# Windowed attention and a GEGLU feed-forward block on one core: residue-class attention with short key blocks, on-chip reciprocals, 512-token FFN chunks, engines ordered by hand

## The chip, the core and the metric

The kernel runs on one core of a Trainium2 chip. The core has a matrix engine (TensorE, PE in the profile, with PEld for its weight loads), three engines for elementwise work (VectorE = DVE, ScalarE = ACT, GpSimd = POOL), a queue engine (SyncE = SP) and 16 DMA engines. Each engine works its own instruction list in order and waits for others by semaphores. TensorE writes only into PSUM, eight banks of 512 float32 per partition; VectorE and ScalarE read it from there. The metric is the device time of one execution in microseconds, lower is better.

## The reference

Attention over 8 batches, 8 heads, 576 positions and 64 channels, then a gated feed-forward block over the 4608 tokens:

```python
window = 32; dilation = 4; scale = 1.0 / np.sqrt(D)
scores = scale * np.matmul(q, k.transpose(0, 1, 3, 2))
rel = pos[:, None] - pos[None, :]
mask_plain = (rel >= 0) & (rel < window)
mask_dil = (rel >= 0) & (rel < window * dilation) & (rel % dilation == 0)
# heads 0 to 3 use mask_plain, heads 4 to 7 mask_dil
attn = softmax(where(mask, scores, -1e9))
x = (attn @ v) as [4608 tokens, 512]
g = x @ w_gate                       # 512 x 1536
gelu = 0.5 * g * (1.0 + erf(g / sqrt(2)))
out = (gelu * (x @ w_val)) @ w_out   # 1536 x 512
```

All inputs and the output are float32. A plain head sees the last 32 positions. A dilated head sees every fourth of the last 128 positions, that is 32 positions of its own residue class modulo 4.

## The kernel before

**Loads.** `emit_loads(b)` (L161) brings q, k and v of a batch in five blocks of 128 positions each through GpSimd's queue, converted to f16 on the way, fifteen DMAs (L169, L177) and some memsets for the padding. `emit_weight_loads` (L84) brings the three weight matrices in one DMA each, between batch 0 and batch 1 in the queue.

**Attention of one batch.** `emit_transposes` (L185) turns q and k of each pair of heads into a channels-by-positions layout with TensorE transposes, five of q and five of k, and ScalarE copies them out of PSUM (L198). For each pair of heads the scores are computed with keys on the partitions (L243 to L251): a block of 128 keys meets 256 queries, since the mask reaches 128 positions back. The two heads of a pair use the upper and the lower 64 rows of the matrix engine. ScalarE takes Exp (L261, L262), VectorE multiplies by a 0/1 mask (L265, L266), and `emit_pv` (L215) multiplies by v, whose 65th column is ones, so that row 64 of the result is the softmax denominator. ScalarE copies the result to `ev` (L227, L271). The denominators then go through DRAM: `dden` (L272), back as a 128x36 tile, reciprocal on VectorE (L291), out again as `drec`, and back as `rec`, replicated over 64 partitions (L297). Eight VectorE multiplications per batch (L304) write the normalised heads into `xT`, a ring that holds four batches.

**FFN.** 18 chunks of 256 tokens. `emit_g1` (L107) computes gate and value for each of 12 blocks of 128 hidden units (8 matmuls of 256 columns each, L114), ScalarE takes Tanh (L122), and two VectorE passes form `u` (L124, L126). `emit_g2` (L130), one chunk later, computes two blocks of 128 tokens against `wo_t` (24 matmuls of 512 columns, L136); ScalarE copies each out (L144) and issues its store (L145).

**Order.** For each batch b the program emits the loads of b+1, the attention of b, then the chunks whose last token lies in batch b-1, then the reciprocals of b. The instructions are given to a scheduler that works by this order and by the availability of buffers; PSUM tiles share seven banks by the tag "S".

Of the kernel before, what the change touches and what calls it, by code (L numbers as in the profile page):

```python
# [10 lines left out]
F16 = mybir.dt.float16  # L12
# [3 lines left out]


def _np_window_pattern(plain: bool, nkeys: int = 128, nq: int = 256, win: int = 32, dil: int = 4):
    kk = np.arange(nkeys)[:, None]
    qq = np.arange(nq)[None, :]  # L20
    rel = qq - kk
    if plain:
        m = (rel >= 0) & (rel < win)
    else:
        m = (rel >= 0) & (rel < win * dil) & (rel % dil == 0)
    return m.astype(np.float16)
# [3 lines left out]
def kernel(  # L30
# [10 lines left out]
    nc = tc.nc  # L41
# [4 lines left out]
    NSB = (S + P - 1) // P  # L46
    SBL = S - (NSB - 1) * P
    NHP = H // 2
    scale = 1.0 / np.sqrt(D)
    CT = float(np.sqrt(2.0 / np.pi))  # L50

    FTOK = 256
    NFC = NT // FTOK
    NNB = DFF // P
    NKC = DM // P
    RB = 4 * S
    CW = H * S // P

    pat_plain = _np_window_pattern(True)
    pat_dil = _np_window_pattern(False)  # L60

    def seg_masks(pat):
        m1 = np.concatenate([pat[:, 0:256], pat[:, 0:256]], axis=1)
        m2 = np.concatenate([pat[:, 0:256], pat[:, 0:192], pat[:, 0:64]], axis=1)
        return m1.astype(np.float16), m2.astype(np.float16)

    m1_p, m2_p = seg_masks(pat_plain)
    m1_d, m2_d = seg_masks(pat_dil)
    m_dram = nc.inline_tensor(np.stack([m1_p, m2_p, m1_d, m2_d]), name="attn_masks")
# [3 lines left out]
    big = ctx.enter_context(tc.tile_pool(name="big", bufs=1))  # L73

    masks = const.tile([P, 4, 512], F16, tag="masks")
    nc.sync.dma_start(masks, m_dram.ap().rearrange("t p c -> p t c"))
    ident = const.tile([P, P], F16, tag="ident")
    nc.sync.dma_start(ident, id_dram.ap())

    wg_t = big.tile([P, NKC, DFF], F16, tag="wg")  # L80
    wv_t = big.tile([P, NKC, DFF], F16, tag="wv")
    wo_t = big.tile([P, NNB, DM], F16, tag="wo")

    def emit_weight_loads():  # L84
        nc.gpsimd.dma_start(out=wg_t, in_=moe_w_gate.rearrange("(kc p) n -> p kc n", p=P))
        nc.gpsimd.dma_start(out=wv_t, in_=moe_w_val.rearrange("(kc p) n -> p kc n", p=P))
        nc.gpsimd.dma_start(out=wo_t, in_=moe_w_out.rearrange("(fc p) m -> p fc m", p=P))

    xT = [big.tile([P, RB], F16, tag=f"xT{i}", name=f"xT{i}") for i in range(NHP)]

    psum = ctx.enter_context(tc.tile_pool(name="psum", bufs=1, space=bass.MemoryType.PSUM))
    qkp = ctx.enter_context(tc.tile_pool(name="qkp", bufs=2))
    qtp = ctx.enter_context(tc.tile_pool(name="qtp", bufs=2))
    prb = ctx.enter_context(tc.tile_pool(name="prb", bufs=8))
    evp = ctx.enter_context(tc.tile_pool(name="evp", bufs=2))
    recp = ctx.enter_context(tc.tile_pool(name="recp", bufs=1))
    cdp = ctx.enter_context(tc.tile_pool(name="cdp", bufs=2))
    dramp = ctx.enter_context(tc.tile_pool(name="dramp", bufs=2, space=bass.MemoryType.DRAM))
    ffn = ctx.enter_context(tc.tile_pool(name="ffn", bufs=3))
    osbp = ctx.enter_context(tc.tile_pool(name="osbp", bufs=4))  # L100
    upool = ctx.enter_context(tc.tile_pool(name="upool", bufs=2 * NNB))

    SB = 7

    u_tiles = {}

    def emit_g1(c):  # L107
        r0 = (c * FTOK) % RB
        us = []
        for nb in range(NNB):  # L110
            mm1 = psum.tile([P, 2, FTOK], F32, tag="S", bufs=SB)
            for gi, w_t in ((0, wg_t), (1, wv_t)):
                for kc in range(NKC):
                    nc.tensor.matmul(  # L114
                        mm1[:, gi, :],
                        w_t[:, kc, ts(nb, P)],
                        xT[kc][:, ds(r0, FTOK)],
                        start=(kc == 0),
                        stop=(kc == NKC - 1),
                    )  # L120
            th = ffn.tile([P, FTOK], F16, tag="th")
            nc.scalar.activation(th, mm1[:, 0, :], AF.Tanh, bias=0.0, scale=CT)  # L122
            tg = ffn.tile([P, FTOK], F16, tag="tg")
            nc.vector.scalar_tensor_tensor(tg, th, 1.0, mm1[:, 0, :], ALU.add, ALU.mult)  # L124
            ut = upool.tile([P, FTOK], F16, tag="u")
            nc.vector.tensor_tensor(ut, tg, mm1[:, 1, :], ALU.mult)  # L126
            us.append(ut)
        u_tiles[c] = us

    def emit_g2(c):  # L130
        t0 = c * FTOK
        us = u_tiles.pop(c)
        for tb in range(FTOK // P):
            fout = psum.tile([P, DM], F32, tag="S", bufs=SB)
            for fc in range(NNB):
                nc.tensor.matmul(  # L136
                    fout,
                    us[fc][:, ts(tb, P)],
                    wo_t[:, fc, :],
                    start=(fc == 0),  # L140
                    stop=(fc == NNB - 1),
                )
            osb = osbp.tile([P, DM], F32, tag="osb")
            nc.scalar.copy(osb, fout)  # L144
            nc.scalar.dma_start(out=out[ds(t0 + tb * P, P), :], in_=osb)  # L145

    ffn_sched = {}
    for c in range(NFC):
        bmax = (FTOK * (c + 1) - 1) // S
        ffn_sched.setdefault(bmax + 1, []).append(c)  # L150
    g2_pending = []

    def emit_chunk(c):
        emit_g1(c)
        if g2_pending:
            emit_g2(g2_pending.pop(0))
        g2_pending.append(c)

    qk_tiles = {}

    def emit_loads(b):  # L161
        q_sb = qkp.tile([P, NSB, H, D], F16, tag="qsb", name=f"qsb{b}")
        k_sb = qkp.tile([P, NSB, H, D], F16, tag="ksb", name=f"ksb{b}")
        vp = qkp.tile([P, H, NSB, 65], F16, tag="vp", name=f"vp{b}")
        for t_sb, t_dr in ((q_sb, q), (k_sb, k)):
            nc.gpsimd.memset(t_sb[SBL:P, NSB - 1, :, :], 0.0)
            for sb in range(NSB):
                npart = P if sb < NSB - 1 else SBL
                nc.gpsimd.dma_start(  # L169
                    out=t_sb[0:npart, sb, :, :],  # L170
                    in_=t_dr[b, :, ds(sb * P, npart), :].rearrange("h p d -> p h d"),
                )
        nc.gpsimd.memset(vp[:, :, :, 64:65], 1.0)
        nc.gpsimd.memset(vp[SBL:P, :, NSB - 1, 0:64], 0.0)
        for kb in range(NSB):
            npart = P if kb < NSB - 1 else SBL
            nc.gpsimd.dma_start(  # L177
                out=vp[0:npart, :, kb, 0:64],
                in_=v[b, :, ds(kb * P, npart), :].rearrange("h p d -> p h d"),
            )  # L180
        qk_tiles[b] = (q_sb, k_sb, vp)

    qkT_tiles = {}

    def emit_transposes(b, group):  # L185
        if b not in qk_tiles:
            return
        q_sb, k_sb, _ = qk_tiles[b]
        if b not in qkT_tiles:
            qkT = qtp.tile([P, 2, NHP, NSB, P], F16, tag="qkT", name=f"qkT{b}")  # L190
            qkT_tiles[b] = qkT
        qkT = qkT_tiles[b]
        for hp in group:
            for qk, src in ((0, q_sb), (1, k_sb)):
                trp = psum.tile([P, NSB, P], F16, tag="S", bufs=SB)
                for sb in range(NSB):
                    nc.tensor.transpose(trp[:, sb, :], src[:, sb, 2 * hp : 2 * hp + 2, :], ident)  # L197
                nc.scalar.copy(qkT[:, qk, hp, :, :], trp)  # L198

    emit_loads(0)  # L200
    emit_weight_loads()
    emit_transposes(0, range(NHP))
    for b in range(B):
        if b + 1 < B:
            emit_loads(b + 1)
        q_sb, k_sb, vp = qk_tiles.pop(b)
        tok0 = (b * S) % RB
        qkT = qkT_tiles.pop(b)

        ev = evp.tile([65, H, S], F32, tag="ev")  # L210
        tailp = psum.tile([65, H, 64], F32, tag="T", bufs=1)
        dden = dramp.tile([H, S], F32, tag="dden")
        drec = dramp.tile([H, S], F32, tag="drec")

        def emit_pv(h, p1, p2):  # L215
            pv = psum.tile([65, 512], F32, tag="S", bufs=SB)
            vph = vp[:, h, :, :]
            nc.tensor.matmul(pv[:, 0:128], vph[:, 0, :], p1[:, 0:128], start=True, stop=False)
            nc.tensor.matmul(pv[:, 128:256], vph[:, 0, :], p1[:, 128:256], start=False, stop=False)
# [10 lines left out]
        for hp in range(NHP):  # L230
# [21 lines left out]
            for args in prev:  # L252
                emit_pv(*args)
# [88 lines left out]
```

## Time and profile before

| | us |
|---|---|
| median of 3 runs | 469.76 (469.54 to 471.47) |
| span of the profiled execution | 467.5 |
| PE busy | 402.5 |
| VectorE busy | 268.7 |
| ScalarE busy | 249.1 |
| GpSimd busy | 117.2 |

The span is the time from the first to the last instruction in one profiled execution. "Busy" adds up the records of an engine; matmul records overlap, so a busy PE is not a PE at its peak. In the lists of groups a row reads: line, engine, operation, output <- inputs, shapes, count | busy us, mean ns of one | idle time before them and what ended it. In the chain of waits a row is start, length, and what ran; in the timeline also the idle time before.

### The profile page before, as it was taken

Reading aid. Unit: us, or ns where it says so; the run is one execution under the profiler, and the core shown is the slowest. Engines: PE = TensorE matmul, PEld = TensorE weight load, DVE = VectorE, ACT = ScalarE, POOL = GpSimd, SP = SyncE. Lnnn points to the kernel's source line nnn. Section 1 sums busy time; section 2 is a strip of 40 time slices with the busy share of each in tenths; the row PEclk is TensorE's granted clock in tenths of the full one; section 3 lists DMA queues with packets and bytes.
Section 4 is the critical chain, followed back from the end, with each engine's and each line's share of the span. In section 5 each row is a group of like instructions: output and inputs, shape, how many; then the busy total and the mean of one; then the engine's idle time right before and its main releaser. Section 6 shows DMA issues by size and latency. Waiting matters only on the chain.

```text
span 467.5 us, 8578 instructions
## 1 busy us (share of the span) xinstructions
PE 402.5 (86%) x3376; PEld 299.6 (64%) x3376; DVE 268.7 (57%) x632; ACT 249.1 (53%) x518; POOL 117.2 (25%) x159
## 2 busy tenths in 40 slices
PE   2750674998899889989999979998999789999996
PEld 1540444984778467947787658765877477777782
DVE  0230127877656856584775658195638765985580
ACT  2761844557636573758345395638555763333332
POOL 9902789460407030701203404000000000000000
PEclk9755655999899989995999999996799989999999
DMA  9999999995649127950853908600041103211002
GB/s 138 143 211 182 172 125 128 75 177 73 43 72 187 50 20 62 197 73 4 54 147 61 108 25 56 149 24 22 5 103 49 45 5 77 72 47 47 22 24 90
DMA packets 123975, 39.29 MB, mean 84 GB/s; under 512 B 115736, under 2 KB 117784, under 8 KB 123416
## 3 DMA queue, kind: packets, MB, share of 16 engines
q0 software_dynamic: 115120, 18.88, 55.3%
q1 hardware_dynamic: 3632, 10.44, 10.2%
q10 hardware_dynamic: 5184, 9.44, 5.7%
q8 instruction: 26, 0.43, 0.4%
q14 instruction: 13, 0.11, 0.1%
HBM read 47.89 MB, written 9.73 MB: 123 GB/s over the span
## 4 chain that ended last, share of the span: by engine, by line
PE 58%; DVE 15%; DMA 11%; ACT 8%; POOL 5%; issue 2%; ACTq 0%; POOLq 0%
PE mm L114 35%; PE fout L136 13%; DVE xT L304 8%; DMA wo_t<-in_moe_w_out_dram 6%; ACT ev L227 3%; DVE ut L126 3%; DVE tg L124 3%; ACT e L261 2%; DMA vp<-in_v_dram 2%; PE trp L197 2%; ACT e L262 2%; DMA rec<-drec 2%; POOL vp L177 2%; POOL ksb L169 1%; DVE p L265 1%
## 5 line engine op out<-in xcount | busy, mean ns | idle before, releaser
L124 DVE SCALAR_TENSOR_TENSOR tg<-th,mm 128x256 f16<-128x256 f16 x216 | 88.0, 419 | 90.2 <-ACT th L122 90.2
L114 PE MATMUL mm<-xT,wg_t 128*128 128x256 f16 x864 | 134.9, 278 | 0.7 <-DVE xT L304 0.7
L114 PE MATMUL mm<-xT,wv_t 128*128 128x256 f16 x864 | 132.3, 277 | 0.0
L122 ACT ACTIVATE th<-mm 128x256 f16<-128x256 f32 x216 | 82.3, 393 | 91.1 <-PE mm L114 70.5
L136 PE MATMUL fout<-wo_t,ut 128*128 128x512 f16 x432 | 96.0, 379 | 0.0
L114 PEld LDWEIGHTS <-wv_t 128*128 128x128 f16 x864 | 85.9, 99 | 12.3 <-issue 0.8
L114 PEld LDWEIGHTS <-wg_t 128*128 128x128 f16 x864 | 85.3, 100 | 11.6
L126 DVE TENSOR_TENSOR ut<-tg,mm 128x256 f16<-128x256 f16 x216 | 86.8, 417 | 4.5
L136 PEld LDWEIGHTS <-ut 128*128 128x128 f16 x432 | 42.3, 98 | 47.3
L144 ACT COPY osb<-fout 128x512 f32<-128x512 f32 x36 | 21.1, 586 | 75.6 <-PE fout L136 65.6
L265 DVE TENSOR_TENSOR p<-e,masks 128x512 f16<-128x512 f16 x64 | 27.2, 425 | 59.0 <-ACT e L261 55.1
L227 ACT COPY ev<-pv 65x512 f32<-65x512 f32 x64 | 37.2, 582 | 25.5 <-PE pv L224 24.2
L304 DVE TENSOR_TENSOR xT<-ev,rec 64x576 f16<-64x576 f32 x64 | 48.0, 750 | 1.0 <-DMA rec<-drec 0.2
L198 ACT COPY qkT<-trp 128x640 f16<-128x640 f16 x64 | 39.5, 729 | 10.2 <-PE trp L197 10.2
L169 POOL DMA_DIRECT2D ksb<-in_k_dram x40 | 33.8, 886 | 22.5 <-DMA wo_t<-in_moe_w_out_dram 6.9
L266 DVE TENSOR_TENSOR p<-e,masks 128x512 f16<-128x512 f16 x64 | 27.1, 424 | 20.0 <-ACT e L262 18.3
L262 ACT ACTIVATE e<-sB 128x512 f16<-128x512 f32 x64 | 38.5, 602 | 0.0
L197 PE MATMUL trp<-ident,qsb 128*128 128x128 f16 x160 | 17.7, 241 | 23.9 <-DMA qsb<-in_q_dram 23.9
L261 ACT ACTIVATE e<-sA 128x512 f16<-128x512 f32 x64 | 38.3, 598 | 0.0
L169 POOL DMA_DIRECT2D qsb<-in_q_dram x40 | 33.8, 876 | 4.9 <-DMA vp<-in_v_dram 4.9
L177 POOL DMA_DIRECT2D vp<-in_v_dram x40 | 33.6, 859 | 0.0
L197 PEld LDWEIGHTS <-qsb 128*128 128x128 f16 x160 | 12.4, 108 | 26.7 <-DMA qsb<-in_q_dram 24.6
(45 smaller groups left out, 386.2 us busy)
## 6 DMA issues: line engine op xcount, KB each, us to landing
rec<-drec SPq DMA_DIRECT2D x8, 1152.0 KB, 8.2
out_dram<-osb ACTq DMA_DIRECT2D x36, 256.0 KB, 2.1
qsb<-in_q_dram POOLq DMA_DIRECT2D x32, 128.0 KB, 5.9
ksb<-in_k_dram POOLq DMA_DIRECT2D x32, 128.0 KB, 4.9
vp<-in_v_dram POOLq DMA_DIRECT2D x32, 128.0 KB, 4.7
wg_t<-in_moe_w_gate_dram POOLq DMA_DIRECT2D x1, 1536.0 KB, 14.0
wv_t<-in_moe_w_val_dram POOLq DMA_DIRECT2D x1, 1536.0 KB, 20.6
wo_t<-in_moe_w_out_dram POOLq DMA_DIRECT2D x1, 1536.0 KB, 27.6
```

The source lines that it names most:

```text
L114: nc.tensor.matmul(mm1[:, gi, :], w_t[:, kc, ts(nb, P)], xT[kc][:, ds(r0, FTOK)], start=(kc == 0), stop=(kc == NKC - 1),)
L122: nc.scalar.activation(th, mm1[:, 0, :], AF.Tanh, bias=0.0, scale=CT)
L124: nc.vector.scalar_tensor_tensor(tg, th, 1.0, mm1[:, 0, :], ALU.add, ALU.mult)
L126: nc.vector.tensor_tensor(ut, tg, mm1[:, 1, :], ALU.mult)
L136: nc.tensor.matmul(fout, us[fc][:, ts(tb, P)], wo_t[:, fc, :], start=(fc == 0), stop=(fc == NNB - 1),)
L169: nc.gpsimd.dma_start(out=t_sb[0:npart, sb, :, :], in_=t_dr[b, :, ds(sb * P, npart), :].rearrange("h p d -> p h d"),)
L177: nc.gpsimd.dma_start(out=vp[0:npart, :, kb, 0:64], in_=v[b, :, ds(kb * P, npart), :].rearrange("h p d -> p h d"),)
L198: nc.scalar.copy(qkT[:, qk, hp, :, :], trp)
L227: nc.scalar.copy(ev[:, h, 0:512], pv)
L261: nc.scalar.activation(e1, sA[i], AF.Exp, bias=0.0, scale=scale)
L262: nc.scalar.activation(e2, sB[i], AF.Exp, bias=0.0, scale=scale)
L304: nc.vector.tensor_tensor(xT[hp][ds(rb, 64), ds(tok0, S)], ev[0:64, h, :], rec[:, h, :], ALU.mult)
```

## The change

The attention part is laid out anew. Plain heads: four blocks of 128 keys against 160 queries, and one block for the last keys against 80. Dilated heads: positions are sorted by residue class modulo 4 while they are loaded and copied, so a class of 144 positions has a band of 32 as well; four blocks of 128 keys against 144 queries and one for the remainder against 72. v gets no 65th column: the denominators come from matmuls with a matrix of ones, which gives them on all 64 partitions of a head. In `emit_pv` and in the transposes the two heads of a pair write to PSUM partitions 0 to 63 and 64 to 127. The reciprocals stay on the chip: `norm_r` transposes the denominators in 32x32 blocks on VectorE, takes 18 reciprocals per partition, and transposes back with each repeated 32 times; `norm_x` multiplies and writes `xT`, which now holds all tokens.

The FFN runs in 9 chunks of 512 tokens, with ScalarE's Gelu and one VectorE pass (`u` scaled by 32, undone in the store, which is on VectorE and SP's queue). PSUM is one tile `ps` of eight banks, used by number. The engines' order is that of the program (`manual_schedule`), and the attention of later batches is placed between the FFN's blocks. The diff, cut to what is new:

```diff
+    ctx.enter_context(tc.manual_schedule())
...
+    def load_qk(b):
+        qm = ldp.tile([P, H, 4, D], F16, tag="qm", name=f"qm{b}")
+        km = ldp.tile([P, H, 4, D], F16, tag="km", name=f"km{b}")
+        rem = ldp.tile([P, H, D], F16, tag="rem", name=f"rem{b}")
+        for t, src in ((qm, q), (km, k)):
+            nc.gpsimd.dma_start(
+                out=t.rearrange("p h r d -> p h (r d)"),
+                in_=src[b, :, 0 : 4 * P, :].rearrange("h (p r) d -> p h (r d)", r=4),
+            )
+        nc.gpsimd.dma_start(out=rem[0:64], in_=q[b, :, 4 * P : S, :].rearrange("h p d -> p h d"))
+        nc.gpsimd.dma_start(out=rem[64:128], in_=k[b, :, 4 * P : S, :].rearrange("h p d -> p h d"))
...
+    def t_q(n, bank, eng_main, eng_rem):
...
+        t_mm(qm, hp, bank)
+        for hl in range(2):
+            nc.tensor.transpose(
+                ps16[64 * hl : 64 * hl + 64, bank, 512:640], rem[:, 2 * hp + hl, :], ident
+            )
+        t_main(n, 0, bank, eng_main)
...
+    def t_mm(src, hp, bank):
+        for r in range(4):
+            for hl in range(2):
+                nc.tensor.transpose(
+                    ps16[64 * hl : 64 * hl + 64, bank, r * P : (r + 1) * P],
+                    src[:, 2 * hp + hl, r, :],
+                    ident,
+                )
...
+    def emit_s(n, b0):
...
+        for j in (0, 1, 4, 2, 3):
+            for hl in range(2):
...
+                nc.tensor.matmul(o, lhs, rhs, start=True, stop=True)
...
+        nc.scalar.activation(pvh[:, :, 0:half], sb[:, 0, :, 0:half], AF.Exp, bias=0.0, scale=scale)
+        nc.scalar.activation(pvh[:, :, half:hw], sb[:, 1, :, 0 : 2 * mw], AF.Exp, bias=0.0, scale=scale)
+        nc.vector.tensor_tensor(pv, pv, mask_p if is_plain(n) else mask_d, ALU.mult)
...
+    def emit_pv(n, b0):
...
+        for bank, c0, c1, j, pc, den, st in mms:
+            for hl in range(2):
...
+                oo = o[bank][64 * hl : 64 * hl + 64]
...
+                nc.tensor.matmul(oap, lhs, rhs, start=st, stop=True, skip_group_check=True)
...
+    def norm_r(n, b0):
+        den = psf[:, b0 * 512 + 960 : b0 * 512 + 1536]
+        dt = nrm.tile([P, 18, 32], F32, tag="dt")
+        nc.vector.transpose(dt.rearrange("p b c -> p (b c)"), den)
+        rc = nrm.tile([P, 18], F32, tag="rc")
+        nc.vector.reciprocal(rc, dt[:, :, 0:1].rearrange("p b c -> p (b c)"))
+        rb = nrm.tile([P, S], F32, tag="rb")
+        nc.vector.transpose(
+            rb.rearrange("p (b c) -> p b c", c=32),
+            bass.AP(tensor=rc.tensor, offset=rc.offset, ap=[rc.ap[0], [1, 18], [0, 32]]),
+        )
...
+    def ffn1(c, nb, b0):
+        tok = slice(c * CH, (c + 1) * CH)
+        ns = slice((nb % 4) * P, (nb % 4 + 1) * P)
+        for gi, w in ((0, wg_t[nb // 4]), (1, wv_t[nb // 4])):
+            for kc in range(NKC):
+                nc.tensor.matmul(
+                    ps[:, b0 + gi, :], w[:, kc, ns], xT[kc][:, tok], start=(kc == 0), stop=(kc == NKC - 1)
+                )
+        g = ffn.tile([P, CH], F16, tag="g")
+        nc.scalar.activation(g, ps[:, b0, :], AF.Gelu)
+        nc.vector.scalar_tensor_tensor(u_t[nb], g, USCALE, ps[:, b0 + 1, :], ALU.mult, ALU.mult)
...
+    load_qk(0)
+    load_v(0)
+    for i in range(3):
+        load_w(i)
+    load_qk(1)
+    for i in range(3):
+        load_wo(i)
+    load_v(1)
+
+    SB, VB, TB = 4, 4, 7
...
+    def t_pair(n, b0):
+        t_q(n, b0, "act", "dve")
+        t_k(n, b0 + 1, "dve")
+
+    def pv_all(n, b0):
+        emit_pv(n, b0)
+        norm_r(n, b0)
+        norm_x(n, b0)
+
+    t_pair(0, 0)
+    t_pair(1, 2)
+    emit_s(0, SB)
+    t_pair(2, 0)
+    t_pair(3, 2)
+    for i in range(1, 4):
+        emit_s(i, SB)
+        pv_all(i - 1, 1)
+    pv_all(3, 1)
+
+    next_t = next_s = next_pv = NHP
+    NU = B * NHP
+    for c in range(NCH):
+        if c + 2 < B:
+            load_qk(c + 2)
+            load_v(c + 2)
+
+        need = min(NU, NHP * (c + 2))
+        t_stop = need if c == 0 else min(NU, NHP * (c + 3))
+        t_list = [(n, t) for n in range(next_t, t_stop) for t in range(2)]
+        next_t = t_stop
+        pv_list = list(range(next_pv, min(next_s, need)))
+        next_pv += len(pv_list)
+        t_slots = {}
+        first = 7 if c == 0 else 2
+        per = -(-len(t_list) // (11 - first))
+        for i, x in enumerate(t_list):
+            t_slots.setdefault(first + i // per, []).append(x)
+        pend = None
         for nb in range(NNB):
...
+            ffn1(c, nb, 0 if nb % 2 == 0 else 2)
+            if pend is not None:
+                norm_x(pend, VB)
+                pend = None
+            if nb in (1, 3, 5, 7) and pv_list:
+                pend = pv_list.pop(0)
+                emit_pv(pend, VB)
+                norm_r(pend, VB)
+            for n, t in t_slots.get(nb, []):
+                if t == 0:
+                    t_q(n, TB, "act", "act")
+                else:
+                    t_k(n, TB, "act")
+
+        s_list = list(range(next_s, next_t))
+        next_s = next_t
+        now_pv = [n for n in s_list if n < need]
...
+        def do_s():
+            if s_list:
+                emit_s(s_list[0], SB)
+                emitted.append(s_list.pop(0))
+
+        def do_pv():
+            if now_pv and now_pv[0] in emitted[:-1]:
+                pv_all(now_pv.pop(0), 1)
+
+        do_s()
+        for tb in range(4):
+            bank = 0 if now_pv else tb
+            ffn2(c, tb, bank)
+            do_s()
+            do_pv()
+            store(c, tb, bank)
+        while s_list:
+            do_s()
+            do_pv()
+        for n in now_pv:
+            pv_all(n, 1)
```

Pairs of heads are numbered n = 4 b + pair. By this program chunk 0 transposes pairs 4 to 7 and does their scores and PV in its second half; chunk 1 transposes pairs 8 to 15, does the scores of all eight in its second half and the PV of 8 to 11; from chunk 2 to chunk 5 a chunk does the PV of four pairs among its ffn1 blocks, transposes four pairs, and does their scores in its second half; chunk 6 does the last four PVs; chunks 7 and 8 are FFN alone.

More of the change, by code (lines that the diff above doesn't have):

```diff
@@ L9 @@
 from concourse._compat import with_exitstack
-from concourse.bass import ds, ts
 F16 = mybir.dt.float16
@@ L77 @@
+    ffn = ctx.enter_context(tc.tile_pool(name="ffn", bufs=3))
+    osbp = ctx.enter_context(tc.tile_pool(name="osbp", bufs=4))
     ident = const.tile([P, P], F16, tag="ident")
     nc.sync.dma_start(ident, id_dram.ap())
[L80 to L109, printed above, removed]
-        for nb in range(NNB):
[L111 to L198, printed above, removed]
@@ L308 @@
-    for c in ffn_sched.get(B, []):
-        emit_chunk(c)
-    while g2_pending:
-        emit_g2(g2_pending.pop(0))
+    mask_p = const.tile([P, 2 * 720], F16, tag="mask_p")
+    nc.sync.dma_start(mask_p, mp_dram.ap())
+    mask_d = const.tile([P, 2 * 648], F16, tag="mask_d")
+    nc.sync.dma_start(mask_d, md_dram.ap())
+    ones = const.tile([P, 64], F16, tag="ones")
+    nc.vector.memset(ones, 1.0)
+    wg_t = [const.tile([P, NKC, CH], F16, tag=f"wg{i}", name=f"wg{i}") for i in range(3)]
+    wv_t = [const.tile([P, NKC, CH], F16, tag=f"wv{i}", name=f"wv{i}") for i in range(3)]
@@ new lines, with load_w @@
+    wo_t = [const.tile([P, 4, DM], F16, tag=f"wo{i}", name=f"wo{i}") for i in range(3)]
+    xT = [const.tile([P, NT], F16, tag=f"xT{i}", name=f"xT{i}") for i in range(NKC)]
+    u_t = [const.tile([P, CH], F16, tag=f"u{i}", name=f"u{i}") for i in range(NNB)]
+    ps = psum.tile([P, 8, 512], F32, tag="ps")
+    psf = ps.rearrange("p b c -> p (b c)")
+    ps16 = psf.bitcast(F16).rearrange("p (b c) -> p b c", b=8)
+    def load_w(i):
+        cs = slice(i * CH, (i + 1) * CH)
+        nc.gpsimd.dma_start(out=wg_t[i], in_=moe_w_gate[:, cs].rearrange("(kc p) n -> p kc n", p=P))
+        nc.gpsimd.dma_start(out=wv_t[i], in_=moe_w_val[:, cs].rearrange("(kc p) n -> p kc n", p=P))
@@ new lines, in t_mm, with t_k, copy @@
+    def t_mm(src, hp, bank):
[5 more added lines that the diff above has]
+                    ident,
+                )
+    def t_k(n, bank, eng_main):
+        b, hp = divmod(n, NHP)
+        qm, km, rem = tiles["qk", b]
+        t_mm(km, hp, bank)
+        t_main(n, 1, bank, eng_main)
+    def copy(eng, dst, src):
+        if eng == "act":
+            nc.scalar.copy(dst, src)
+        else:
+            nc.vector.tensor_copy(dst, src)
@@ new lines, in t_main, with geom @@
+    def t_main(n, t, bank, eng):
+        qk = tiles["qkT", n]
+        src = ps16[:, bank, 0:512].rearrange("p (r i) -> p r i", r=4)
+        if is_plain(n):
+            dst = qk[:, t, 0 : 4 * P].rearrange("p (i r) -> p r i", r=4)
+        elif t == 0:
+            dst = qk[:, t, :].rearrange("p (r i) -> p r i", r=4)[:, :, 0:P]
+        else:
+            dst = qk[:, t, 0 : 4 * P].rearrange("p (r i) -> p r i", r=4)
+        copy(eng, dst, src)
+    def geom(n):
+        mw, tw = (160, 80) if is_plain(n) else (144, 72)
+        off = [0, mw, 2 * mw + tw, 3 * mw + tw, 2 * mw]
+        return mw, tw, off, 4 * mw + tw
@@ new lines, in ffn2, with store @@
+    def ffn2(c, tb, bank):
+        for fc in range(NNB):
+            nc.tensor.matmul(
+                ps[:, bank, :],
+                u_t[fc][:, tb * P : (tb + 1) * P],
+                wo_t[fc // 4][:, fc % 4, :],
+                start=(fc == 0),
+                stop=(fc == NNB - 1),
+            )
+    def store(c, tb, bank, eng="dve"):
+        osb = osbp.tile([P, DM], F32, tag="osb")
+        if eng == "act":
+            nc.scalar.activation(osb, ps[:, bank, :], AF.Copy, bias=0.0, scale=1.0 / USCALE)
+        else:
+            nc.vector.tensor_scalar(osb, ps[:, bank, :], 1.0 / USCALE, None, ALU.mult)
+        t0 = c * CH + tb * P
+        nc.sync.dma_start(out=out[t0 : t0 + P, :], in_=osb)
```

295 lines of the change are left out of this document (165 added, 130 removed).

## The prediction

> **What bounds the kernel now.** The page's slices come first: they show where the engines work at all.
>
> ```profile
> span 467.5 us, 8578 instructions
> ...
> PE   2750674998899889989999979998999789999996
> ...
> PEclk9755655999899989995999999996799989999999
> DMA  9999999995649127950853908600041103211002
> GB/s 138 143 211 182 172 125 128 75 177 73 43 72 187 50 20 62 197 73 4 54 147 61 108 25 56 149 24 22 5 103 49 45 5 77 72 47 47 22 24 90
> ```
>
> TensorE (PE) is ragged and slow-clocked for seven slices of 11.7 us, and full afterwards. The windows view puts numbers on it; its columns are the stretch, its length, busy us of PE, PEld, DVE, ACT, POOL, then granted clock, DMA share, GB/s.
>
> ```profile
> 0.00:76.00 76.00, 36.62 (x281) 24.89 (x282) 17.22 (x36) 40.39 (x64) 50.07 (x70) 0.65 1.71 159
> 76.00:463.80 387.80, 365.86 (x3095) 274.74 (x3094) 251.45 (x597) 208.17 (x453) 67.11 (x90) 0.95 0.53 69
> 463.80:467.50 3.70, 0.00 (x0) 0.00 (x0) 0.00 (x0) 0.59 (x1) 0.00 (x0) 0.77 0.19 71
> ```
>
> The chain of waits (start, length, what) names the pieces.
>
> ```profile
> 51.75 11.27 DMA vp<-in_v_dram
> ...
> 69.12 0.49 ACT e L262
> ...
> 70.56 0.66 DVE xT L304
> ...
> 79.39 1.30 PE mm L114 x8
> ...
> 235.40 10.48 PE mm L114 x96
> 245.88 5.18 PE fout L136 x24
> 251.06 2.23 PE trp L197 x40
> ```
>
> FFN starts at 79.4: batch 1's attention stands ahead of it in PE's order and waits for batch 1's v, behind the weights in the DMA queue. From there the 18 chunks need 18 x (10.48 + 5.18) = 281.9 us, and the end is PE's at 463.8. The other 463.8 - 79.4 - 281.9 = 102.5 us are six attention phases (batches 2 to 7), 17.1 each, 2.23 of it transposes. So PE's order is the bound, in three parts: 79.4 start, 282 FFN, 102 attention that stands between chunks; 3.7 of store follow. The measured median is 2.3 us above the span (469.76 against 467.5).
>
> **The change, part by part.** Durations and pitches come from these groups (by shape) and pieces of the timeline.
>
> ```profile
> L124 DVE SCALAR_TENSOR_TENSOR tg<-th,mm 128x256 f16<-128x256 f16 x216 | 88.0, 419 | 90.2 <-ACT th L122 90.2
> L265 DVE TENSOR_TENSOR p<-e,masks 128x512 f16<-128x512 f16 x64 | 27.2, 425 | 59.0 <-ACT e L261 55.1 <-PE pv L224 2.2
> L304 DVE TENSOR_TENSOR xT<-ev,rec 64x576 f16<-64x576 f32 x64 | 48.0, 750 | 1.0 <-DMA rec<-drec 0.2
> L291 DVE RECIPROCAL crec<-cden 128x36 f32<-128x36 f32 x8 | 3.0, 372 | 11.4 <-DMA cden<-dden 11.4
> L198 ACT COPY qkT<-trp 128x640 f16<-128x640 f16 x64 | 39.5, 729 | 10.2 <-PE trp L197 10.2
> L262 ACT ACTIVATE e<-sB 128x512 f16<-128x512 f32 x64 | 38.5, 602 | 0.0
> L144 ACT COPY osb<-fout 128x512 f32<-128x512 f32 x36 | 21.1, 586 | 75.6 <-PE fout L136 65.6 <-DMA out_dram<-osb 10.0
> L198 ACT ACT_TABLE_LOAD x1 | 1.3, 1283 | 0.8 <-PEq L326 0.8
> L226 PEld LDWEIGHTS <-vp 128*65 128x65 f16 x64 | 9.3, 145 | 1.1 <-issue 1.1
> ```
>
> ```profile
> 204.77 0.28 PE L243 MATMUL sA<-qkT 64*128 64x256 f16 x2
> 204.89 0.27 PE L245 MATMUL sA<-qkT 64*128 64x256 f16 x2
> ...
> 208.16 0.22 PE L224 MATMUL pv<-p,vp 128*65 128x128 f16 x1
> 208.22 0.19 PE L225 MATMUL tailp<-p,vp 128*65 128x64 f16 x1
> 208.25 0.20 PE L226 MATMUL tailp<-p,vp 128*65 128x64 f16 x1
> ```
>
> *FFN.* 512-token chunks stream the same columns: 9 x (96 + 48) matmuls of 512 at 5.18/24 = 0.216 is 279.9 us, 31.1 a chunk, 1.73 for one ffn1 block. Gelu replaces Tanh plus one VectorE pass. L124 (419 for 256) and L304 (750 for 576) give VectorE 0.15 us fixed and 1.03 ns an element, and L265 half of that per element for f16 in SBUF. So a block costs about 0.60 on ScalarE (L262) and 0.68 on VectorE, both under 1.73: hidden by PE. If they weren't, PE would wait for PSUM in all 108 blocks; 1.28 a block is no cost on PE.
>
> *Start.* No batch-1 attention stands before chunk 0. Ten POOL loads instead of fifteen bring batch 0, in packets four times as long for q, k and half of v. The first rows today:
>
> ```profile
> 1.28 4.34 POOL qsb L169 x5
> ...
> 5.96 0.29 PE L197 MATMUL trp<-ident,qsb 128*128 128x128 f16 x1 [5.96 <-DMA qsb<-in_q_dram]
> ...
> 16.76 27.64 DMA wo_t<-in_moe_w_out_dram
> ```
>
> A load of 128 KB lands 4.7 after its issue begins (1.28 to 5.96). With no memset ahead the first begins at 0.75, but it is now 512 KB: at some 200 GB/s (the slices with the long weight packets) q's main part is there at 7.4, k's at 10.0 and the remainder rows, which stand behind both in the queue, at 10.4. Transposes and copies of two pairs (0.73 a copy, PE at half clock) put the first scores at 13; Exp, mask and the copies of pairs 2 and 3, which free PV's banks, put PV 0 at 18. Then each of the four pairs of heads costs PV (1.2 at half clock) plus normalising before the next PV may reuse its three banks. Normalising is two 32x32 VectorE transposes of 576, a reciprocal and a multiply, each needing the one before: 0.75 + 0.26 + 0.76 + 0.75 and three hand-overs of 0.04, 2.65. Four times about 4.2 after 18 is 35. The weights are in time: 1.8 MB of batch 0 and the first thirds of gate and value, 1.1 MB, are through by 25 at 140 to 200 GB/s. Bounds 28 (VectorE passes overlap) to 41 (each transpose at half rate, 1.35; no row shows it, I take L124's rate because it is the nearest PSUM pass).
>
> *Attention on PE.* A pair costs 18 transposes, 10 score matmuls, 24 PV matmuls. Scores (720 columns in two row halves) run as the pairs of L243 do, two at one start, 256 columns per 0.11: 0.30. Transposes and PV put the two heads in column halves instead; before has none of that. If halves run together as row halves do: 9 x 0.035 x 2 = 0.63 and 1408 columns or 0.6 plus switching, 0.75. If one after the other: 1.05 and 1.25. I take the first, since the row halves are the nearest row. On the path: 28 pairs of transposes x 0.63 = 17.6, 20 PVs x 0.75 (chunks 2 to 6) and 16 scores x 0.30 with 0.5 a chunk for the first Exp: 21.8. Bound above +23.
>
> *Transposes of chunks 0 and 1.* They come in twos on bank 7: k waits until ScalarE has copied q's 512 and the remainder. From L198 (729 for 640): 0.60 + 0.25 + hand-overs, 1.2 in which PE stands at k's first transpose with the next ffn1 block queued behind it, for 4 + 8 pairs: 14.4. From chunk 2 on an ffn1 block of 1.73 lies between: hidden.
>
> *Second half of chunks 0 and 1.* This is the new wait. While `now_pv` is not empty every ffn2 block uses bank 0 alone, and its VectorE store stands in the queue behind mask(n+1) and the whole normalising of n. From the score start: scores and drain 0.4, two Exps over 800 and 640 elements 1.45 (L262: 0.60 long for 512, 0.49 in the chain where the next follows: 0.07 to 0.17 fixed and 0.83 ns an element), mask of 1440 0.90, normalising 2.65, store 0.69, hand-overs: 6.25 us in which PE has 1.05 of work. Who waits: the next ffn2 block at the head of PE's queue, and all behind it. Three such gaps in each chunk, with heads of 0.3 and tails of 3.9 (PV and normalising of the last pair before chunk 1 may read it) and 6.2 (three further scores, one Exp each): 6 x 6.25 + 0.6 + 10.1 = 48.2. Chunks 2 to 5 have four ffn2 banks and no PV there, so nothing of it.
>
> *Clock.* Stages with gaps lose it:
>
> ```profile
> 205.00:220.00 15.00, 12.24 (x117) 9.23 (x112) 8.72 (x19) 12.56 (x25) 0.15 (x1) 0.66 0.05 20
> 253.00:268.00 15.00, 15.00 (x123) 11.55 (x121) 8.21 (x24) 8.33 (x19) 9.31 (x12) 1.00 1.27 89
> 268.00:283.00 15.00, 11.96 (x134) 8.46 (x133) 6.88 (x17) 13.39 (x27) 1.24 (x3) 1.00 0.09 34
> ```
>
> An attention phase with PE 82% busy fell to 0.66, another at 80% did not. PE will be near 40% busy in these stages, so I let 6 ffn2 blocks of 2.6 run at half clock for most of their length, +2.15 each, and the starts of chunks 0, 1, 2 lose 2, 1.5 and 2: 18.4. Bounds 5.5 and 21.
>
> *Queues.* SP loses the four DMAs of the reciprocals and takes the stores from ScalarE's queue, 36 for 32; the round trip lay beside FFN chunks, so nothing is credited beyond the phases above. POOL's loads of batch c+2 are issued at chunk c, over a chunk before their transposes; with a mean DMA share of 0.53 in the long window they hide, and would cost PE their landing time if buffers came free late.
>
> *Table loads.* Exp and Gelu alternate in six chunks: 13 loads x 1.28 on ScalarE, those before Gelu hidden by the last ffn2 block (2.6), those before Exp nearly so; the 0.5 above is what sticks out. The Trainium skill, "ScalarE: Activation LUTs", What ACT_TABLE_LOAD costs, gives the same 1283 ns but adds a drain of about 1380; by it the sum would be some 8 us higher.
>
> *Sum.* 35 + 279.9 + 17.6 + 14.4 + 21.8 + 48.2 + 18.4 + 3.7 (tail as now) = 439.0 span, against 467.5; with 2.3 the time is 441.
>
> **Rivals.** *Column halves run one after the other*: +11.8 for transposes (28 x 0.42), +10 for PV (20 x 0.5), and a little at the start: 464. Against it: row halves overlap.
>
> *The clock stays up*: -12.9 from the ffn2 blocks: 428. For it: 268 to 283. Against it: those gaps were about 1 us, these are 5.
>
> *Weight loads of the column halves are not covered* (slower): the 65-column loads take 145 ns where 128-column ones take 99, though L225 to L226 follow in 0.03, so today they hide. If each of the 28 x 18 + 20 x 24 = 984 exposed half-width matmuls had a pitch of its load's shortest 0.11 instead of 0.033, the kernel would take 441 + 76 = 517. It decides from 441 + 26 = 467, a pitch of 60 ns.
>
> ```profile
> L114 PEld LDWEIGHTS <-wv_t 128*128 128x128 f16 x864 | 85.9, 99 | 12.3 <-issue 0.8
> 162.29 0.11 PEld L220 LDWEIGHTS <-vp 128*65 128x65 f16 x1
> ```
>
> The Trainium skill, "TensorEngine Tiling (Array Packing)", Gotcha 2, says that column tiling is exclusive with Fast Weight Load, which speaks for this rival; the 145 against 99 (both at mixed clocks) agrees with a slower path for narrow weights, and no run here shows column halves yet.
>
> *The new FFN is not faster*: it isn't in my sum either; 280 against 282 is all that it gives, so the gain must come from start and attention.
>
> **How the numbers follow.** Forecast 0.50 (430 to 452), serial halves 0.19 (452 to 467), clock up or a shorter start 0.19 (410 to 430), uncovered loads 0.09 (over 472), between 467 and 472 0.03. About 0.5% is what a measurement of this kernel can tell from no change. Faster 0.88, same 0.03, slower 0.09. Leaving out the shortest starts and the uncovered loads, the range is 418 to 467.
>
> **What would show it.** First ffn1 near 35; chunks 2 to 5 near 38 each and 7 and 8 at 31.1; in chunks 0 and 1 PE idle some 5 us before each ffn2 block, released by the store, with the clock near half; PV matmuls of two heads with one start. Wrong if PV pairs start 0.07 apart, if chunks 2 to 5 take over 42, or if PE waits there for VectorE.

## The result and the profile after

The changed kernel takes 451.14 us (median of 4 runs, 450.90 to 451.33) against 470.57 beside it; the ratio is 0.9606, interval 0.9572 to 0.9641. The profiled execution has a span of 449.5. The slices of the page, one of 11.2 us each:

```profile
span 449.5 us, 7001 instructions
...
PE   0637975556777555799999999999999999999996
...
PEclk9955999668999988899999999999999999999999
```

The ragged part ran to slice 7 before; now it runs to slice 17, with two dips (slices 7 to 9 and 14 to 16, half busy) and 6 to 7 tenths between them. The chain of waits gives their places (start, length, what):

```profile
37.44 1.44 DVE xT L320
38.93 15.83 PE ps L332 x61
...
110.68 4.69 PE ps L332 x21
...
188.62 4.68 PE ps L332 x16
...
229.53 3.45 PE ps L332 x16
...
348.61 3.45 PE ps L332 x16
...
383.62 20.72 PE ps L332 x96
404.34 10.36 PE ps L341 x48
...
445.82 0.69 DVE osb L354
```

L332 is ffn1, L341 ffn2. Read as stages, beside what the terms of the prediction give when they are sorted by chunk:

| stage | from | length | by the prediction's terms |
|---|---|---|---|
| start | 0 | 38.9 | 35 |
| chunk 0 | 38.9 | 71.8 | 69.8 |
| chunk 1 | 110.7 | 77.9 | 78.9 |
| chunks 2 to 5 | 188.6 | 160.0 | 155.2 |
| chunk 6 | 348.6 | 35.0 | 34.1 |
| chunks 7 and 8 | 383.6 | 62.2 | 62.2 |
| tail | 445.8 | 3.7 | 3.7 |

The balance against before: the time to the first ffn1 block whose inputs are complete went from 79.4 to 38.9 (-40.5), the FFN's own matmuls from 281.9 to 279.9 (-2.0), and everything else between start and tail, which is attention on PE's path with its waits and lost clock, from 102.5 to 449.5 - 38.9 - 279.9 - 3.7 = 127.0 (+24.5). The sum is -18.0, the difference of the spans. So the start brings the gain and more, and over half of that is given back later. Most of the 127.0 is in chunks 0 and 1, which take 40.7 and 46.8 more than a pure chunk of 31.1. Which part of the change shortens the start, the new order or the new attention, no run separates.

What chunks 0 and 1 wait for stands in the list of waits (engine, line, whom it waited for, us in total, times, longest):

```profile
PE ps L341 <- DVE osb L354: 29.8, 6, 5.3
...
PE ps L170 <- ACT qkT L184: 14.4, 12, 1.5
```

The first is the six ffn2 blocks that wait for the store of the block before. One of them in the timeline (start, length, engine, line, what; the idle time before it in brackets):

```profile
73.19 0.49 PE L228 MATMUL ps<-qkT 64*128 64x160 f16 x10
...
73.97 0.51 PE L297 MATMUL ps<-P,ones 128*64 128x64 f16 x12
...
75.18 0.91 DVE L236 TENSOR_TENSOR P<-P,mask_p 128x1440 f16<-128x1440 f16 x1 [1.58 <-ACT P L235]
76.00 0.78 DVE L302 STREAM_TRANSPOSE dt<-ps 128x576 f32<-128x576 f32 x1
76.81 0.27 DVE L304 RECIPROCAL rc<-dt 128x18 f32<-128x18 f32 x1
77.11 0.78 DVE L306 STREAM_TRANSPOSE rb<-rc 128x576 f32<-128x576 f32 x1
77.93 0.76 DVE L317 TENSOR_TENSOR xT<-ps,rb 128x576 f16<-128x576 f32 x1
78.60 0.68 DVE L354 TENSOR_SCALAR osb<-ps 128x512 f32<-128x512 f32 x1
79.34 5.28 PE L341 MATMUL ps<-wo,u 128*128 128x512 f16 x12 [4.85 <-DVE osb L354]
```

From the scores at 73.19 to ffn2 at 79.34 pass 6.15 us, in which VectorE works through a mask, a normalising and at last the store, although the block to be stored was ready at 73.3. And the block that follows takes 5.28 instead of 2.70. The windows view of the block before the gap and of the one behind it has the granted clock in its third column from the end:

```profile
70.56:73.26 2.70, 2.70 (x15) 1.10 (x16) 0.95 (x2) 2.08 (x3) 2.70 (x5) 1.00 1.31 173
79.34:84.62 5.28, 5.28 (x14) 1.69 (x15) 0.00 (x0) 0.00 (x0) 0.00 (x0) 0.50 0.53 100
```

The clock fell to half, and the matmuls run at half the rate. The other five blocks behind such gaps take 4.05 to 4.99 us at clocks of 0.54 to 0.67.

### The profile page after: what moved, and what is told of

It is laid out like the page before. It is cut to its first block, busy times and chain, and to the rows that moved or that the text cites. A ratio compares the mean times of both kernels' runs of the same rounds, so it can differ in the third digit from the quotient of the medians.

```text
span 449.5 us, 7001 instructions
## 1 busy us (share of the span) xinstructions
PE 369.9 (82%) x2960; PEld 177.7 (40%) x2960; DVE 218.5 (49%) x315; ACT 184.0 (41%) x288; POOL 69.1 (15%) x93
## 4 chain that ended last, share of the span: by engine, by line
PE 78%; DVE 12%; ACT 6%; DMA 2%; issue 1%; POOL 1%; DVEq 0%; POOLq 0%
PE ps L332 43%; PE ps L341 24%; PE ps L170 5%; PE ps L297 4%; ACT qkT L184 3%; PE ps L228 3%; DVE rb L306 2%; DVE xT L320 2%; DVE dt L302 2%; DMA rem<-in_k_dram 2%; DVE P L236 2%; ACT P L234 1%; DVE osb L354 1%; ACT P L235 1%; DVE xT L317 1%; DVE rc L304 1%
## 5 line engine op out<-in xcount | busy, mean ns | idle before, releaser
L341 PE MATMUL ps<-wo,u 128*128 128x512 f16 x432 | 108.6, 409 | 29.8 <-DVE osb L354 29.8
L337 DVE SCALAR_TENSOR_TENSOR u<-g,ps 128x512 f16<-128x512 f16 x108 | 74.3, 688 | 113.4 <-PE ps L332 106.1
L332 PE MATMUL ps<-xT,wg 128*128 128x512 f16 x432 | 114.3, 387 | 5.0 <-DVE xT L320 4.7
L336 ACT ACTIVATE g<-ps 128x512 f16<-128x512 f32 x108 | 65.7, 608 | 127.2 <-PE ps L332 125.0
L332 PE MATMUL ps<-xT,wv 128*128 128x512 f16 x432 | 112.7, 384 | 0.0
L184 ACT COPY qkT<-ps 128x512 f16<-128x512 f16 (+2 forms) x102 | 61.0, 668 | 48.8 <-PE ps L152 28.1
L341 PEld LDWEIGHTS <-u 128*128 128x128 f16 x432 | 43.3, 104 | 85.4 <-issue 43.3
L332 PEld LDWEIGHTS <-wv 128*128 128x128 f16 x432 | 42.8, 99 | 57.7 <-issue 5.6
L234 ACT ACTIVATE P<-ps 128x800 f16<-128x800 f32 (+1 forms) x32 | 25.7, 804 | 74.3 <-PE ps L228 74.2
L332 PEld LDWEIGHTS <-wg 128*128 128x128 f16 x432 | 38.4, 99 | 44.9 <-issue 3.0
L354 DVE TENSOR_SCALAR osb<-ps 128x512 f32<-128x512 f32 x36 | 24.5, 689 | 27.1 <-PE ps L341 27.1
L236 DVE TENSOR_TENSOR P<-P,mask_d 128x1296 f16<-128x1296 f16 x16 | 13.2, 831 | 38.7 <-ACT P L235 38.7
L170 PE MATMUL ps<-ident,km 128*64 128x128 f16 x256 | 14.0, 232 | 14.4 <-ACT qkT L184 14.4
L320 DVE TENSOR_TENSOR xT<-ps,rb 128x576 f16<-128x576 f32 x16 | 23.0, 1436 | 0.2
## 6 DMA issues: line engine op xcount, KB each, us to landing
wo<-in_moe_w_out_dram POOLq DMA_DIRECT2D x3, 512.0 KB, 16.2
```

Source lines behind the costliest of these rows:

```text
L170: nc.tensor.transpose(ps16[64 * hl : 64 * hl + 64, bank, r * P : (r + 1) * P], src[:, 2 * hp + hl, r, :], ident,)
L184: nc.scalar.copy(dst, src)
L234: nc.scalar.activation(pvh[:, :, 0:half], sb[:, 0, :, 0:half], AF.Exp, bias=0.0, scale=scale)
L236: nc.vector.tensor_tensor(pv, pv, mask_p if is_plain(n) else mask_d, ALU.mult)
L320: nc.vector.tensor_tensor(dst.rearrange("p (i b s) -> p b s i", b=2, s=2), num, rb.rearrange("p (b s i) -> p b s i", b=2, s=2), ALU.mult,)
L332: nc.tensor.matmul(ps[:, b0 + gi, :], w[:, kc, ns], xT[kc][:, tok], start=(kc == 0), stop=(kc == NKC - 1))
```

## The experiments

All times are medians; the kernel before ran beside them at 469.7 to 471.1, with single runs from 463.5 to 472.4, so the comparisons that count are those with the changed kernel, 451.14, or with another experiment.

**e1: the stores first.** The order of emission on VectorE only:

```diff
             ffn2(c, tb, bank)
+            store(c, tb, bank)
             do_s()
             do_pv()
-            store(c, tb, bank)
```

> Only VectorE's order changes: each store is issued before the mask and the normalising that follow its ffn2 block. Theory (in chunks 0 and 1 PE stands before each ffn2 block until the store has come through VectorE's queue, 4.8 us a time, and loses its clock there): the six periods of 9 to 11 us fall to what VectorE needs for one pair, store 0.69, mask 0.9, normalising 2.7 to 3.3, so 4.3 to 5, and ffn2 is back at 2.7; the two chunks lose about 31 us together and the time is 415 to 425. Rival (the gap belongs to the attention chain of score, Exp, mask, PV, normalising, and PE would stand elsewhere): within 5 us of 451.

Measured 418.68 (ratio to before 0.8918, interval 0.8864 to 0.8972). In its timeline the store directly follows its block, and ffn2 keeps its length:

```profile
72.62 0.68 DVE L354 TENSOR_SCALAR osb<-ps 128x512 f32<-128x512 f32 x1
...
73.52 2.76 PE L341 MATMUL ps<-wo,u 128*128 128x512 f16 x12
...
78.59 2.76 PE L341 MATMUL ps<-wo,u 128*128 128x512 f16 x12
```

No wait of ffn2 for a store is left in its list. From the first ffn2 block at 69.6 to the third at 78.6 pass 9.0 us, two periods; in the changed kernel these two take 8.8 and 11.3. The theory holds: 32 us hung on the place of one `store` call in VectorE's queue.

**e5 and e9: the clock.** The waits stay, but PE is given work in them, ten (e5) or eighteen (e9) matmuls in each of six gaps, whose results nobody uses:

```diff
             do_s()
             do_pv()
+            if c < 2 and tb < 3:
+                for _ in range(10):
+                    nc.tensor.matmul(ps[:, SB, :], ident, wg_t[0][:, 0, :], start=True, stop=True)
             store(c, tb, bank)
```

> The changed kernel with ten extra matmuls of 512 columns (results unused, into a score bank that is free then) in each of the six gaps of chunks 0 and 1, after the Exp and ahead of the next ffn2 block; the waits for the store stay. Theory (the ffn2 blocks of 4.1 to 5.3 us against 2.7 elsewhere, 27.3 against 16.2 for the six, are long only because the clock falls in the gaps): blocks of 2.7 and 440. Rival (they are long for another reason, weights or PSUM): blocks as before and 451 or a little more.

> As e5, with 18 extra matmuls instead of ten in each gap, so that PE has under 1 us of idle time left before the ffn2 block where it had 2.3 to 2.9. In e5 the first block of each chunk came back to 2.75 and the other four stayed at 4.2 to 4.4. Theory (the clock falls with idle time): all six at 2.7 to 2.8 and 440 to 442. Rival (those four are long for another reason): as e5, 447 or more.

e5 took 446.74, between its two expectations. Its timeline shows both outcomes:

```profile
78.34 2.75 PE L341 MATMUL ps<-wo,u 128*128 128x512 f16 x12 [2.42 <-DVE osb L354]
...
86.94 4.44 PE L341 MATMUL ps<-wo,u 128*128 128x512 f16 x12 [2.29 <-DVE osb L354]
```

Nearly equal gaps, other lengths: only the first of the three blocks in each chunk came back. By the windows view those two ran at a granted clock of 1.00 and the other four at 0.62 to 0.64, so the slow blocks are slow by their clock; but the idle time just before a block doesn't alone decide it. e9 fills the gaps further. It took 441.78, and all six blocks stand at 2.75:

```profile
82.34 4.04 PE L447 MATMUL ps<-wg,ident 128*128 128x512 f16 x18
86.95 2.75 PE L341 MATMUL ps<-wo,u 128*128 128x512 f16 x12 [0.56 <-DVE osb L354]
```

All six have a granted clock of 1.00. The kernel gains 9.4 us with the waits in place: the six blocks give back 10.8, but the ffn1 blocks at the start of chunk 1 now take 6.38 instead of 4.69. In e1 such starts lose as well (7.42 for chunk 1 and 5.36 for chunk 2, against 4.69 and 4.68). So some 8 to 9 of e1's 32 us are clock, an estimate from these two runs, and the remainder is the waiting.

**e2: two banks for the transposes of chunks 0 and 1.**

```diff
-                    t_k(n, TB, "act")
+                    t_k(n, TB if c > 1 else TB - 1, "act")
```

> In chunks 0 and 1 the k transposes go to bank 6 instead of waiting for bank 7. Theory (PE waits 14.4 us in 12 places for ScalarE to empty bank 7): 435 to 439. Rival (ScalarE becomes the bound, since a slot of a plain pair has copies of 1.4 and 1.3 and a Gelu of 0.6 against 2.6 on PE): half of it comes back as waits of the next transposes, 442 to 446.

Measured 437.22 (0.9321, interval 0.9259 to 0.9383), 13.9 less. The wait of 14.4 us is down to

```profile
PE ps L170 <- ACT qkT L184: 1.5, 6, 0.3
```

The rival shows only in places: where two plain pairs follow each other the chain runs over ScalarE's copies for some microseconds, but PE has little to wait.

**e3: dense writes.** The same elements in another order, for the dilated `norm_x`, and likewise for the plain copies of q and k:

```diff
-                dst.rearrange("p (i b s) -> p b s i", b=2, s=2),
-                num,
-                rb.rearrange("p (b s i) -> p b s i", b=2, s=2),
+                dst.rearrange("p (i b s) -> p i b s", b=2, s=2),
+                num.rearrange("p b s i -> p i b s"),
+                rb.rearrange("p (b s i) -> p i b s", b=2, s=2),
```

> The dilated normalising multiply and the plain q and k copies take the same elements in another order, so that writes are dense in SBUF and reads strided in PSUM. Theory (the f16 writes of 2 bytes at steps of 8 bytes double the pass, 1.44 against 0.75 and 1.30 against 0.58): multiply 0.75, copies 0.6, and on the path 6 x 0.68 + 6 x 0.7 + 1.5 at the start, 441. Rival (a stepped pattern costs the same on the read side, or the four-dimensional pattern is what costs): durations and time as before, 451.

Measured 443.86 (0.9454, interval 0.9396 to 0.9511). The groups by shape, of the changed kernel and then of e3 (count | busy us, mean ns of one | idle before):

```profile
L184 ACT COPY qkT<-ps 128x512 f16<-128x512 f16 x60 | 56.3, 945 | 48.8 <-PE ps L152 28.1 <-PE ps L170 20.6
...
L320 DVE TENSOR_TENSOR xT<-ps,rb 128x576 f16<-128x576 f32 x16 | 23.0, 1436 | 0.2
...
L317 DVE TENSOR_TENSOR xT<-ps,rb 128x576 f16<-128x576 f32 x16 | 12.1, 753 | 0.2
```

```profile
L184 ACT COPY qkT<-ps 128x512 f16<-128x512 f16 x60 | 35.1, 587 | 54.1 <-PE ps L152 30.9 <-PE ps L170 23.2
...
L321 DVE TENSOR_TENSOR xT<-ps,rb 128x576 f16<-128x576 f32 x16 | 17.9, 1119 | 0.2
```

ScalarE's copies behave as the theory says, 945 to 587 (half of them were already dense). VectorE's multiply only falls from 1436 to 1119, not to 753, so both accounts hold in part. Whether its stepped reads or the four-dimensional pattern keeps it there, and by which of its two inputs, no run separates. Of the 7.3 us, 2.8 are the start (36.1 against 38.9) and 3.9 the wait for bank 7 (10.5 against 14.4).

**e6 and e7: together.** e6 has the edits of e1, e2 and e3; e7 also loads the remainder rows of q and k before the main parts:

```diff
+        nc.gpsimd.dma_start(out=rem[0:64], in_=q[b, :, 4 * P : S, :].rearrange("h p d -> p h d"))
+        nc.gpsimd.dma_start(out=rem[64:128], in_=k[b, :, 4 * P : S, :].rearrange("h p d -> p h d"))
         for t, src in ((qm, q), (km, k)):
...
-        nc.gpsimd.dma_start(out=rem[0:64], in_=q[b, :, 4 * P : S, :].rearrange("h p d -> p h d"))
-        nc.gpsimd.dma_start(out=rem[64:128], in_=k[b, :, 4 * P : S, :].rearrange("h p d -> p h d"))
```

> Stores first, two banks for the transposes of chunks 0 and 1, and dense writes, together. If the three waits are separate: 418.7, less 13.9 for the banks, less some 3 of the 7 for the writes (the shorter copies are already hidden behind the second bank): 399 to 404. If they cover each other (the store order already hid what the second bank saves): 410 or more.

> As the one before, and the remainder rows of q and k are loaded ahead of the main parts. Theory (the start waits for the remainder, which landed at 13.2 where 10.4 was forecast): 1 to 3 us less. Rival (k's main part lands as late, so the start stays): within 0.5 us.

e6 took 399.61 (0.8500, interval 0.8453 to 0.8547), e7 398.04 (0.8478, interval 0.8444 to 0.8513). The three savings nearly add up: 53.7 apart, 51.5 together. The 1.6 us of e7 is at the edge of what the runs tell apart (397.53 to 399.36 against 397.58 to 400.46). Its start in the chain is 35.3, in e6 36.3 and in the changed kernel 38.9, so the order of the loads gives about 1 us at most, no more than the landing of the remainder rows varies from run to run (12.3 to 13.7); the chain now waits for k's main part, which lands at 12.2. In e7 chunks 0 and 1 take 47.3 and 51.8:

```profile
35.30:82.60 47.30, 42.07 (x352) 20.09 (x352) 24.84 (x36) 20.01 (x36) 17.91 (x23) 0.93 1.26 154
82.60:134.40 51.80, 46.89 (x462) 23.36 (x462) 26.46 (x39) 27.77 (x56) 15.53 (x20) 0.93 0.77 93
```

**e10: the stores of chunks 0 and 1 on ScalarE**, otherwise e7:

```diff
-            store(c, tb, bank)
+            store(c, tb, bank, "act" if bank == 0 and c < 2 else "dve")
```

> As e7, and the stores of chunks 0 and 1 go to ScalarE. Theory (after e1 the period of a pair, 4.5 us, is VectorE's: store 0.69, mask 0.83 to 0.91, normalising 2.65 to 3.0): each of the six periods loses up to 0.7, down to PE's own 3.8, 394 to 396. Rival (PE or the Exps already set the period): 398.

Measured 397.47: the rival's number. The store was not on e7's path. The chain there goes from ffn2 through scores, Exps, mask, normalising and PV to the next ffn2, and the first store runs while VectorE waits for the Exps. The timeline of e7:

```profile
64.37 0.68 DVE L355 TENSOR_SCALAR osb<-ps 128x512 f32<-128x512 f32 x1
...
66.01 0.91 DVE L237 TENSOR_TENSOR P<-P,mask_p 128x1440 f16<-128x1440 f16 x1 [0.95 <-ACT P L236]
```

In e10 the store stands ahead of the Exps in ScalarE's queue, and so in the chain:

```profile
64.00 0.60 ACT osb L353
64.60 0.73 ACT P L235
65.33 0.61 ACT P L236
...
65.96 0.91 DVE P L237
```

Counted from the first ffn2 block (61.33 in e7, 61.20 in e10) this mask starts after 4.68 and 4.76, and the third ffn2 block after 9.00 and 9.08. So VectorE's work alone doesn't set the period; the whole chain does.

**e4: the column halves one after the other.**

```diff
-        for bank, c0, c1, j, pc, den, st in mms:
-            for hl in range(2):
+        for hl in range(2):
+            for bank, c0, c1, j, pc, den, st in mms:
```

and the same exchange in `t_mm`.

> Same matmuls, but all of head A's in the lower column half first, then all of head B's, in PV and in the transposes. Theory (neighbours in different column halves overlap): one after the other they take twice as long, 0.56 more for each of 20 PVs on the path and 0.48 more for each of 28 pairs of transposes, 25 us, time 476. Rival (the order doesn't matter, the halves never overlapped or the array reorders them): 451.

Measured 462.40 (0.9851, interval 0.9778 to 0.9924), 11 more than the changed kernel, between the expectations. In the chain, the changed kernel first:

```profile
193.29 0.76 PE ps L297 x24
194.05 1.83 PE ps L332 x8
195.88 0.34 PE ps L170 x8
```

and e4:

```profile
195.93 1.19 PE ps L297 x24
197.11 1.83 PE ps L332 x8
198.95 0.35 PE ps L170 x8
```

PV grew from 0.76 to 1.19, nearly the 1.25 of the prediction's serial case; 20 x 0.43 is 8.6 of the 11. Transposes didn't grow at all. The timeline of e4 suggests why: its records mix, with k transposes, which stand later in PE's list, between the last PV matmuls:

```profile
202.04 0.23 PE L297 MATMUL ps<-P,ones 128*64 128x160 f16 x1
202.06 0.22 PE L170 MATMUL ps<-ident,km 128*64 128x128 f16 x1
202.12 0.23 PE L297 MATMUL ps<-P,ones 128*64 128x160 f16 x1
```

By these start times PE takes matmuls of a free column half ahead of waiting ones, over a distance that covers four transposes but not twelve PV matmuls. That the halves overlap is shown; how far ahead PE looks is only read from these two cases.

**e8: the FFN's arithmetic alone, in the kernel before.** Gelu and one pass; the halving of `wo_t` (L275) goes too:

```diff
-            nc.scalar.activation(th, mm1[:, 0, :], AF.Tanh, bias=0.0, scale=CT)
-            tg = ffn.tile([P, FTOK], F16, tag="tg")
-            nc.vector.scalar_tensor_tensor(tg, th, 1.0, mm1[:, 0, :], ALU.add, ALU.mult)
+            nc.scalar.activation(th, mm1[:, 0, :], AF.Gelu)
...
-            nc.vector.tensor_tensor(ut, tg, mm1[:, 1, :], ALU.mult)
+            nc.vector.tensor_tensor(ut, th, mm1[:, 1, :], ALU.mult)
```

> The kernel before with only the FFN's arithmetic changed: ScalarE's Gelu and one VectorE pass in place of Tanh and two. Theory (VectorE and ScalarE are hidden by PE in the FFN, so this part of the change gives nothing): 464 to 474. Rival A (the second VectorE pass was on the path): under 462. Rival B (Exp and Gelu alternate while attention and FFN overlap, and the table loads cost): over 476.

Measured 476.63 (1.0148, interval 1.0108 to 1.0188): just in rival B's range. VectorE's busy time falls from 268.7 to 188.8, and the kernel is slower; the list of groups has the table loads that came:

```profile
L122 ACT ACT_TABLE_LOAD x7 | 9.0, 1283 | 0.1
L259 ACT ACT_TABLE_LOAD x6 | 7.7, 1283 | 0.1
```

That these loads cause the 7 us is argued from their count, not shown. The profiled run also has a lower granted clock, 0.877 against 0.900, and PE's busy time is 410.4 against 402.5; whether that comes of the loads stays open. What is shown is that this part of the change has no gain of its own in the kernel before.

## Why the prediction was right, and where its terms were off

It named 441 within 418 to 467; 451.14 came, 10 us above the forecast and at the upper edge of its likeliest stretch, 430 to 452. Of a forecast gain of 29 us, 19 came. By its own steps:

*FFN.* Right to 0.1: chunks 7 and 8 take 62.2, and VectorE and ScalarE never hold PE there (PE is busy for 62.16 of the 62.20).

*Start, 35.* Measured 38.9. Two sizes failed. The remainder rows were put at 10.4 and landed at 13.2: the chain has their DMA from 3.80 for 9.43 us, and in the profiles of the other runs with this load order they land between 12.3 and 13.7. And the dilated multiply was priced at 0.75, as the plain one, and takes 1.44 (L320 above), twice on the way to the first chunk. The two 32x32 transposes (0.78 each), the reciprocal (0.27) and the plain multiply (0.75) were within 0.03 of their estimates; the half-rate bound of 1.35 is out.

*Column halves.* Right: the halves overlap, PV at 0.76 was put at 0.75; e4 shows what the first rival would have cost PV. The third rival, uncovered weight loads, is out with the same rows: 24 matmuls in 0.76 us are 32 ns each, where it needed 60.

*Chunks 2 to 5, 38.3.* Measured 39.7 (40.9 the first). VectorE holds no PE there. The missing 1.4 is at the joints: an ffn1 block between transposes or PVs takes 1.83 in the chain and 20.72 / 12 = 1.73 in a pure chunk, an ffn2 block between scores 2.70 against 10.36 / 4 = 2.59. So each turn to half arrays and back costs PE about 0.1, thirteen times a chunk. The prediction had this as "plus switching" for PV alone. The Trainium skill, "TensorEngine Tiling (Array Packing)", Key Properties, says that changing the tiling mode drains TensorE; the trace agrees, with 0.10 and 0.11.

*Bank 7.* 14.4 forecast, 14.4 measured in 12 places, and e2 took 13.9 of it away. That the sum fits so well is partly luck, since it hides two kinds of wait: a plain pair's copies take 1.40 together, since their writes are stepped, and not 0.85; the dilated pairs take 0.82. Forecast were 1.2 for each pair, and the two kinds average out.

*Second half of chunks 0 and 1.* Right in mechanism and size: 6.25 from scores to ffn2 forecast, 6.15 in the gap shown, and the six gaps in the chain last 5.85 to 6.45; e1 removes them. The prediction took the wait as given; that the order on one queue alone makes it, and that the kernel is at 418.7 without it, is from e1.

*Clock.* 12.9 forecast for six ffn2 blocks, 27.3 - 16.2 = 11.1 in the trace, and e9 takes 10.8 of it away (9.4 of its time). The second rival (the clock stays up) is out. The starts of chunks 0, 1 and 2 lost 2.7, 0.2 and 1.2 where 2, 1.5 and 2 were put.

*Table loads.* 13 in the FFN and attention, as counted. The sum with 0.5 a chunk was the nearer one: after an Exp that ends at 189.57 the load starts at 189.59 and Gelu at 190.88.

```profile
188.92 0.65 ACT L235 ACTIVATE P<-ps 128x576 f16<-128x576 f32 x1
...
189.59 1.28 ACT L336 ACT_TABLE_LOAD   x1
...
190.88 0.60 ACT L336 ACTIVATE g<-ps 128x512 f16<-128x512 f32 x1
```

The drain of about 1380 ns that the Trainium skill adds ("ScalarE: Activation LUTs", What ACT_TABLE_LOAD costs) isn't in these rows: the switch takes 1.31 in all.

*The sum.* 439.0 against 449.5: start +3.9, chunk 0 +2.0, chunk 1 -1.0, chunks 2 to 5 +4.8, chunk 6 +0.9. No mechanism was missing; the landing of the remainder rows, the stepped f16 writes and the joints were mis-sized.

## What to carry to other kernels

Order by hand means each queue, not only PE: put what frees a PSUM buffer ahead of what merely comes next, since one store behind a normalising chain cost 32 us, about a quarter of that as lost clock by estimate. Where two producers share one bank, count the emptying copy as PE time, and write f16 densely, leaving the steps to the reading side. A large change is best read as stages against its own pure stage (31.1 us here): chunks 0 and 1, which stood out, held 50.6 of the 53 us that lie between 451 and 398.

## What the hardware showed that was not expected

- Behind idle stretches of 2.3 to 2.9 us, with 2.3 us of extra matmuls ahead of them, ffn2 ran at a granted clock of 0.62 to 0.64 in four of six cases and at 1.00 in two (e5); behind 0.6 to 1.2 us, with 4.0 us of extra matmuls, at 1.00 in six of six (e9). Which of the two, the idle time or the work before it, decides is open.
- f16 writes at steps of 8 bytes: 1436 against 753 ns for 576 elements on VectorE, and about 1300 against 587 for 512 on ScalarE (worked out: its mean is 945, and half of its copies are the dense ones of 587). Stepped PSUM reads cost ScalarE nothing that shows (587), but VectorE's multiply with two stepped inputs, in a four-dimensional pattern, took 1119.
- By the start times of its records, PE starts matmuls of a free column half ahead of others in its list (e4).
